# Layer 2: one block of W2 loaded as 96 rows in three padded groups and 32 rows apart

## The chip, the cores and the metric

The kernel runs on one core of a Trainium2 chip. The metric is device time in microseconds (us) of one execution. Runs of the kernel before: 1343.65, 1343.77 and 1344.35 us, median 1343.77 us.

## The reference

One token goes through two equal layers; each layer is attention over a cache of 8192 keys for 32 heads of 128, and then an MLP. All data is float32.

```
def _A_ref(x, k_cache, v_cache, wq, wo):
    q = (x @ wq).reshape(B, Sq, H, Dh).transpose(0, 2, 1, 3)      # H = 32, Dh = 128, D = 640
    scores = jnp.einsum("bhqd,bhkd->bhqk", q, k_cache) * (Dh ** -0.5)
    p = _softmax(scores, axis=-1)
    o = jnp.einsum("bhqk,bhkd->bhqd", p, v_cache)
    return o.transpose(0, 2, 1, 3).reshape(B, Sq, H * Dh) @ wo
def _B_ref(x, w1, w2):
    h = jnp.maximum(jnp.einsum("bsd,df->bsf", x, w1), 0)          # Dff = 1728
    return jnp.einsum("bsf,fd->bsd", h, w2)

x = x + _A_ref(_layernorm(x), A_k_cache, A_v_cache, A_wq, A_wo)
x = x + _B_ref(_layernorm(x), B_w1, B_w2)
x = x + _A_ref(_layernorm(x), A_k_cache, A_v_cache, A_wq, A_wo)
x = x + _B_ref(_layernorm(x), B_w1, B_w2)
```

## The kernel before

The caches do not fit in the on-chip memory, so nearly all of K and V is read from device memory twice, once per layer. The loads are issued from SP's queue, in an order written out by hand (UNITS, HEADS), into one large tile named ring. `pump` (from L179) issues the next load of K or V as soon as a place in the ring is free; `release` frees a place once TensorE has used it. The weights wq and wo come over ACT's queue.

The second weight matrix of the MLP, W2, is cut by rows into 14 blocks: blocks 0 to 12 are 128 rows by 640 columns (2560 bytes in each row), and block 13 (FB - 1) is packed into 128 rows by 320. `W2_LOADS` groups the blocks into transfers, one list for each layer. In the second layer (index 1 in the code) there are six: blocks 4, 5, 6; blocks 0 to 3; blocks 7, 8, 9; blocks 10, 11; block 12; block 13. `pump` issues them after the last piece of K and V, through `part_of_w2` (from L218), and they all go to SP's queue, so they are the last bytes that the kernel loads. Each has 128 rows.

A transfer waits before its issue for a semaphore named DMAHW0 to DMAHW7. There are eight, used in turn, so a transfer waits until the one that last used its semaphore has landed.

The end of the program is the MLP of the second layer (`mlp`). The hidden values are turned into columns (hT), and then `product(b)` multiplies the column of one block by this block of W2: four matmuls over 128x160 (L482) for blocks 0 to 12, four at L935 for block 13. The profile counts each such matmul as two instructions. The order is that of `W2_LOADS`: seven blocks (4, 5, 6, 0, 1, 2, 3), then some small matmuls for the layer norm (L961, L969, L391), then 7, 8, 9, then one matmul for the spread (L404), then 10, 11, 12, 13. One VectorE operation (L998) adds up, and SP stores the result (L1045).

Of the kernel before, what the change touches and what calls it, by code (L numbers as in the profile page):

```python
# [15 lines left out]
P = 128  # L16
D = 640
# [80 lines left out]
def wide(kind, piece):  # L98

    return 4 * piece[2] * (1 if kind == "k" else DH) // 8  # L100


def size(u):
    return sum(wide(kind, piece) for _, kind, piece in UNITS[u[0]][u[1]])
# [6 lines left out]
FB = 4 * F_TILES + F_REST  # L111
SLOTS = 7
W2_UNITS = SLOTS * D // 8
W2_LOADS = [
    [(0, 1, 2, 3), (4, 5, 6), (7,), (8, 9, FB - 1), (10,), (11,), (12,)],
    [(4, 5, 6), (0, 1, 2, 3), (7, 8, 9), (10, 11), (12,), (FB - 1,)],
]
W2_LAST = 2 * (F_ROWS[2] - P * F_TILES)
assert 2 * W2_LAST == P


def w2_width(blocks):
    return sum(D // 2 if b == FB - 1 else D for b in blocks)


@with_exitstack
def decode_kernel(ctx: ExitStack, tc: tile.TileContext, x, kv, wq, wo, wqo, w1, w2, out):
    nc = tc.nc
    consts = ctx.enter_context(tc.tile_pool(name="consts", bufs=1))
    wts = ctx.enter_context(tc.tile_pool(name="wts", bufs=1))  # L130
# [20 lines left out]
    dram_at, o = {}, 0  # L151
# [8 lines left out]
    def place(layer, u, n):  # L160


        step = 8 if u in KEPT else max(m for m in (8, 64, 256, 512) if n % m == 0)
        low, high = 0, FLAT if u[0] >= 28 else 3 * BIG
        if layer and (u[0] >= 28 or u[0] < HG):
            high = RING
        if n > FLAT // 3:
            step, high = BIG, 3 * BIG
        if layer == 0 and u in kept and (u in KEPT or u[0] == 30 and UNITS[30][u[1]][0][1] == "k"):
            low, high = (EDGE, RING) if u in KEPT else (FLAT, EDGE)  # L170
        at, best = low, None
        for a, m in sorted(live.values()) + [(high, 0)]:
            a = min(a, high)
            if a - at >= n and (best is None or a - at < best[1]):
                best = at, a - at
            at = max(at, -(-(a + m) // step) * step)
        return None if best is None else best[0]

    def pump():  # L179
        while todo:  # L180
            layer, u = todo[0]
            n = size(u)
            at = place(layer, u, n)
            if at is None:
                return
            todo.pop(0)
            o = dram_at[u]
            stays = PARK_ROW if (layer, u) == (1, PARKED) else 0
            nc.sync.dma_start(
                ring[:, 8 * at + stays : 8 * (at + n)],  # L190
                kv[o : o + 8 * P * n].rearrange("(p m) -> p m", p=P)[:, stays:],
            )
            if stays:
                for a, bank in parked:
                    nc.scalar.copy(ring[:, 8 * at + a : 8 * at + a + bank.shape[1]], bank)
            for t, (_, kind, piece) in enumerate(UNITS[u[0]][u[1]]):
                m = wide(kind, piece)
                live[layer, u, t] = at, m
                at_of[layer, u, t] = ring, 8 * at
                at += m  # L200
            if not todo or layer < todo[0][0]:
                assert all(a + m <= RING for a, m in live.values())
                live["w2"] = RING, W2_UNITS
                for part in W2_LOADS[layer][:2]:
                    part_of_w2(layer, part, by_parts[:, part[0] * D :])
                if layer == 0:
                    part_of_w2(0, W2_LOADS[0][2], wct.rearrange("p c d -> p (c d)"))
        rest = W2_LOADS[1][2:]
        if (1, rest[0][0]) not in w2_block:
            n = w2_width(sum(rest, ()))  # L210
            at = place(1, (0, None), n // 8)
            if at is not None:
                at *= 8
                for part in rest:
                    part_of_w2(1, part, ring[:, at:])
                    at += w2_width(part)

    def part_of_w2(L, blocks, where):  # L218
        loads = W2_LOADS[L]
        o = P * w2_width(sum(loads[: loads.index(blocks)], ()))  # L220
        n = w2_width(blocks)
        nc.sync.dma_start(where[:, :n], w2[L, o : o + P * n].rearrange("(p m) -> p m", p=P))
        at = 0
        for b in blocks:
            m = w2_width((b,))
            w2_block[L, b] = where[:, at : at + m]
            at += m
# [20 lines left out]
    def release(L, u, t):  # L248
        if (L or u not in kept) and at_of[key(L, u, t)][0] is ring:
            del live[key(L, u, t)]  # L250
            pump()
        if (L, u, t) in lent:
            lent.remove((L, u, t))
            if not lent:
                del live["w2"]
                pump()
# [35 lines left out]
    load_wq(0, nc.sync)  # L292
    nc.scalar.dma_start(xr, x)
    pump()
    load_wo(0, 0, nc.sync)

# [12 lines left out]
    blocks = ident.rearrange("p (g r) -> p g r", g=4)[:, :, :4]  # L309
# [574 lines left out]
    def mlp(L, o, last, xp, ph):  # L884
# [43 lines left out]
        def product(b):  # L928
# [4 lines left out]
            for g in range(4):  # L933
                rows = slice(W2_LAST * (g // 2), W2_LAST * (g // 2 + 1))
                nc.tensor.matmul(  # L935
                    po[32 * g : 32 * g + 32, :DR],
                    hT[rows, b : b + 1].to_broadcast([W2_LAST, 32]),
                    wt[rows, g % 2 * DR : (g % 2 + 1) * DR],
# [117 lines left out]
def _hidden_rows():  # L1056

    b = [[F_AT[g] + j * P + np.arange(P) for g in range(4)] for j in range(F_TILES)]
    rest = [F_AT[g] + np.arange(F_TILES * P, F_ROWS[g]) for g in range(4)]
    blocks = [x for row in b for x in row]  # L1060
    blocks.append(np.concatenate(rest[:2]))
    blocks.append(np.concatenate(rest[2:] + [-np.ones(P - len(rest[2]) - len(rest[3]), int)]))
    return blocks


def _laid_out(A_x, A_k_cache, A_v_cache, A_wq, A_wo, B_w1, B_w2):
    k = np.asarray(A_k_cache)[0].reshape(H, 4, 4, RUN, DH).transpose(0, 4, 1, 2, 3)
    v = np.asarray(A_v_cache)[0].reshape(H, 4, 4, NBL, 4, 32, DH).transpose(0, 1, 5, 3, 4, 2, 6)
    v = v.reshape(H, P, NBL, 4, 4, DH)
    kv = np.empty(H * P * SK * 2, k.dtype)  # L1070
    o = 0
    for u in ORDER:
        n = 8 * size(u)
        block = kv[o : o + P * n].reshape(P, n)
        o += P * n
        a = 0
        for h, kind, piece in UNITS[u[0]][u[1]]:
            if kind == "k":
                r, c, m = piece
                part = k[h, :, :, r, c : c + m]  # L1080
            else:
                b, r, m = piece
                part = v[h, :, b, :, r : r + m]
            part = part.reshape(P, -1)
            block[:, a : a + part.shape[1]] = part
            a += part.shape[1]
    w2 = np.zeros((P, FB, D), np.asarray(B_w2).dtype)
    for b, f in enumerate(_hidden_rows()):
        w2[f >= 0, b] = np.asarray(B_w2)[f[f >= 0]][:, _COLS]
    w2[W2_LAST:, -1, : D // 2] = w2[:W2_LAST, -1, D // 2 :]  # L1090
    wq = np.asarray(A_wq).reshape(NB, P, NG, HG * DH).transpose(2, 1, 0, 3).reshape(NG, P, HG * D)
    wo = np.asarray(A_wo)[:, _COLS].reshape(NG, HG, DH, D).transpose(0, 2, 1, 3)
    wqo = [
        [np.concatenate([wq[b], wo[a].reshape(P, HG * D)], 1) for a, b in zip(gs[1:-1], gs[2:])]
        for gs in GROUPS
    ]
    return {
        "x": np.repeat(np.asarray(A_x).reshape(D)[_COLS].reshape(4, DR), 32, axis=0),
        "kv": kv,
        "wq": wq.reshape(NG * P, HG * D),  # L1100
        "wo": wo,
        "wqo": np.array(wqo),
        "w1": np.asarray(B_w1).reshape(NB, P, DFF).transpose(1, 0, 2),
        "w2": np.array(
            [
                np.concatenate(
                    [
                        np.concatenate([w2[:, b, : w2_width((b,))] for b in part], 1).reshape(-1)
                        for part in loads
                    ]  # L1110
                )
                for loads in W2_LOADS
            ]
        ),
    }


# [22 lines left out]
```

## Time and profile before

| what | value |
|---|---|
| runs | 1343.65, 1343.77, 1344.35 us |
| span of the profiled execution, first to last instruction | 1340.6 us |
| median of the runs less this span | 3.2 us |
| bytes read from device memory | 570.83 MB, 426 GB/s over the span |
| TensorE busy, VectorE busy | 65%, 22% of the span |
| the chain that ended last, by engine | DMA 67%, PE 27%, DVE 4% |

For the profiled execution the page gives the span and no separate total, so the 3.2 us stand for what lies around the span. The DMA share in a stretch is the mean busy share of the core's 16 DMA engines: 0.50 means that eight engines' worth of work was done. In a list of DMA issues the last number is the time from the issue to the landing of the whole transfer.

### The profile page before, as it was taken

To read this page: it belongs to the slowest core of one execution; us is meant where nothing else is said; L and a number is where in the kernel's file an instruction comes from. 1 tells how busy PE (TensorE), PEld (TensorE's weight loads), DVE (VectorE), ACT (ScalarE), POOL (GpSimd) and SP (SyncE) were. 2 spreads that over 40 slices of the span, in tenths; PEclk is the share of its full clock that TensorE was granted. 3 is DMA by queue.
4 is the path that set the end of the run, shared out by engine and by line. 5 is a ranking of instruction groups with operands and counts; after the bars stand their busy time and mean duration, and the time that the engine had idled before them with its cause. 6 is when DMAs were issued, how large, how long until landed. Compare 5 with 4: busy or idle time off the path is not lost.

```text
span 1340.6 us, 13403 instructions
## 1 busy us (share of the span) xinstructions
PE 874.0 (65%) x5806; PEld 255.5 (19%) x5806; DVE 290.2 (22%) x956; ACT 62.6 (5%) x155; POOL 2.9 (0%) x10
## 2 busy tenths in 40 slices
PE   5463575767657656676688755657566666567687
PEld 2110121111111111112243211112111111111123
DVE  2120121211212112223123212221221212212222
ACT  0000000000000000000000000000000000000000
POOL 0000000000000000000000000000000000000000
PEclk8686787988777887788799977887778787888789
DMA  9999999999999999999999999999999999999998
GB/s 395 431 435 430 442 423 437 429 428 437 432 434 429 428 439 426 433 425 415 425 396 425 430 435 433 432 433 431 433 429 434 432 428 433 437 427 436 425 424 333
DMA packets 24546, 571.70 MB, mean 426 GB/s; under 512 B 2724, under 2 KB 2984, under 8 KB 6952
## 3 DMA queue, kind: packets, MB, share of 16 engines
q1 hardware_dynamic: 21464, 529.31, 92.1%
q10 hardware_dynamic: 3024, 41.53, 7.3%
q8 instruction: 46, 0.75, 0.2%
q14 instruction: 12, 0.10, 0.0%
HBM read 570.83 MB, written 0.00 MB: 426 GB/s over the span
## 4 chain that ended last, share of the span: by engine, by line
DMA 67%; PE 27%; DVE 4%; ACT 1%; issue 1%; SPq 0%; ACTq 0%; DVEq 0%
DMA ring<-in_kv 66%; PE ps L516 10%; PE outs L570 9%; PE side L672 1%; DMA ring<-in_w 1%; DVE p L591 1%; PE acc L621 1%; PE side L440 1%; ACT p L545 1%; DVE h_t L531 1%; PE small L536 1%; PE small L604 1%; PE side L454 1%; DVE p L552 0%; DVE h_t L537 0%
## 5 line engine op out<-in xcount | busy, mean ns | idle before, releaser
L516 PE MATMUL ps<-ring,spread_q 128*32 128x512 f32 (+3 forms) x2088 | 332.7, 727 | 149.2 <-DMA ring<-in_kv 148.6
L570 PE MATMUL outs<-ring,p 128*4 128x512 f32 (+3 forms) x2080 | 310.6, 732 | 164.1 <-DMA ring<-in_kv 95.7
L531 DVE TENSOR_REDUCE h_t<-ps 128x1 f32<-128x512 f32 x64 | 44.3, 691 | 365.4 <-PE ps L516 365.4
L570 PEld LDWEIGHTS outs<-ring,p 128*4 128x4 f32 x2080 | 50.6, 95 | 348.4 <-issue 233.8
L516 PEld LDWEIGHTS ps<-ring,spread_q 128*32 128x32 f32 x2088 | 63.9, 124 | 277.5 <-issue 188.8
L545 ACT ACTIVATE p<-ps,h_t 128x512 f32<-128x512 f32 x63 | 43.3, 687 | 1161.2 <-DVE h_t L537 1161.2
L552 DVE STREAM_TRANSPOSE p<-p 128x128 f32<-128x128 f32 x256 | 79.8, 312 | 63.9 <-ACT p L545 57.2
L587 DVE TENSOR_SCALAR p<-outs,ind 128x128 f32<-128x128 f32 x64 | 22.5, 351 | 317.2 <-PE outs L570 317.2
L604 PE MATMUL small<-ones,p 128*128 128x1 f32 (+1 forms) x128 | 25.3, 267 | 97.4 <-DVE p L591 97.4
L591 DVE SCALAR_TENSOR_TENSOR p<-outs,ind,p 128x128 f32<-128x128 f32 x188 | 66.0, 351 | 6.7
L536 PE MATMUL small<-ident,h_t 128*128 128x128 f32 x128 | 32.7, 339 | 40.1 <-DVE h_t L531 39.9
L604 PEld LDWEIGHTS small<-ones,p 128*128 128x128 f32 x128 | 19.9, 195 | 159.7 <-DVE p L591 158.9
L672 PE MATMUL side<-w_t,wct 128*128 128x448 f32 (+1 forms) x80 | 45.3, 651 | 0.0
L452 DVE TENSOR_SCALAR q_row<-side,ln_r 128x128 f32<-128x128 f32 x56 | 19.5, 349 | 106.0 <-PE ps L516 59.0
L440 PE MATMUL side<-both_t,ln_xc 128*32 128x512 f32 x140 | 37.3, 844 | 0.0
L536 PEld LDWEIGHTS small<-ident,h_t 128*128 128x128 f32 x128 | 20.0, 196 | 89.0 <-DVE h_t L531 85.5
L621 PE MATMUL acc<-both_t,o_cols 128*64 128x320 f32 x220 | 34.6, 458 | 0.0
L454 PEld LDWEIGHTS side<-sel,q_row 128*128 128x128 f32 x112 | 19.3, 216 | 56.3 <-DVE q_row L452 29.9
L537 DVE TENSOR_REDUCE h_t<-small 128x1 f32<-128x128 f32 x64 | 18.7, 292 | 35.4 <-PE small L536 35.4
L454 PE MATMUL side<-sel,q_row 128*128 128x1 f32 x112 | 24.1, 284 | 0.3 <-DVE q_row L452 0.2
L621 PEld LDWEIGHTS acc<-both_t,o_cols 128*64 128x64 f32 x220 | 15.5, 147 | 29.4 <-issue 17.7
L672 PEld LDWEIGHTS side<-w_t,wct 128*128 128x128 f32 x80 | 13.5, 211 | 32.4 <-issue 32.4
(148 smaller groups left out, 219.5 us busy)
## 6 DMA issues: line engine op xcount, KB each, us to landing
ring<-in_kv SPq DMA_DIRECT2D x50, 6144.0 KB, 35.0
ring<-in_kv SPq DMA_DIRECT2D x23, 4096.0 KB, 33.2
ring<-in_kv SPq DMA_DIRECT2D x29, 2048.0 KB, 27.7
both_t<-in_wqo ACTq DMA_DIRECT2D x12, 2560.0 KB, 24.7
ring<-in_kv SPq DMA_DIRECT2D x4, 5120.0 KB, 34.6
ring<-in_kv SPq DMA_DIRECT2D x9, 1024.0 KB, 23.9
w_t<-in_w ACTq DMA_DIRECT2D x1, 4320.0 KB
ring<-in_kv SPq DMA_DIRECT2D x5, 768.0 KB, 29.5
```

The source lines that it names most:

```text
L440: nc.tensor.matmul(pq[32 * strip : 32 * strip + 32], xc[:, c : c + 1].to_broadcast([P, 32]), wq_t[:, c], start=c < 4, stop=c in (1, 2, 3, ...
L454: nc.tensor.matmul(mine[:, :1], row, one_of_each, start=True, stop=True, skip_group_check=True)
L516: nc.tensor.matmul(hd.ps[32 * g : 32 * g + 32, c : c + n], spread_q[:, 3 - r : 35 - r], tile_of[:, at + g * n : at + (g + 1) * n], start=f ...
L531: nc.vector.tensor_reduce(hd.nm, hd.ps, AX.X, ALU.max, negate=True)
L536: nc.tensor.matmul(pt[:, :P], hd.nm.to_broadcast([P, P]), ident, start=True, stop=True)
L545: nc.scalar.activation(hd.p, hd.ps, AF.Exp, bias=hd.low, scale=scale, accum_out=hd.l)
L552: nc.vector.transpose(hd.all_p[:, b * P : (b + 1) * P], hd.p[:, b * P : (b + 1) * P])
L570: nc.tensor.matmul((hd.out if r0 < 2 else hd.out_2)[32 * g : 32 * g + 4, r0:r1].rearrange("p r d -> p (r d)"), hd.all_p[:, 32 * i : 32 * i ...
L591: nc.vector.scalar_tensor_tensor(oc, hd.out[:, r], ind[:, r : r + 1], oc, op0=ALU.mult, op1=ALU.add)
L604: nc.tensor.matmul(pt[:, :n], part, mask.to_broadcast([P, n]), start=i == 0, stop=i == len(parts) - 1,)
L621: nc.tensor.matmul(acc[64 * g : 64 * g + 64, : 2 * DR], col.to_broadcast([P, 64]), wt[:, 2 * DR * g : 2 * DR * (g + 1)], start=first, stop ...
L672: nc.tensor.matmul(pt[:, :n], wct[:, c], w1_t[:, c, f : f + n], start=(c == 0), stop=(c == NB - 1),)
```

## The change

The first transfer of layer 2's W2 (blocks 4, 5, 6) is cut into block 4 alone and blocks 5, 6. Block 4 is then loaded by two transfers. The first carries rows 0 to 95, from a new array w2_front of three lines; each line holds 32 rows and 64 padding values, so that the lines do not run into one another and the source has three as its outermost size. The second carries rows 96 to 127. Destination, values and the order of the products stay the same. `W2_FIRST` says how many transfers go to the fixed place: two in layer 1, three in layer 2.

```
 W2_LOADS = [
     [(0, 1, 2, 3), (4, 5, 6), (7,), (8, 9, FB - 1), (10,), (11,), (12,)],
-    [(4, 5, 6), (0, 1, 2, 3), (7, 8, 9), (10, 11), (12,), (FB - 1,)],
+    [(4,), (5, 6), (0, 1, 2, 3), (7, 8, 9), (10, 11), (12,), (FB - 1,)],
 ]
+W2_FIRST = [2, 3]
+FRONT = 3
+FRONT_ROWS = 32 * FRONT
+FRONT_GAP = 64
...
-                for part in W2_LOADS[layer][:2]:
+                for part in W2_LOADS[layer][: W2_FIRST[layer]]:
                     part_of_w2(layer, part, by_parts[:, part[0] * D :])
...
-        nc.sync.dma_start(where[:, :n], w2[L, o : o + P * n].rearrange("(p m) -> p m", p=P))
+        if L and blocks == loads[0]:
+            nc.sync.dma_start(
+                where[:FRONT_ROWS, :n],
+                w2_front[:, : 32 * n].rearrange("g (r m) -> g r m", m=n),
+            )
+            o += FRONT_ROWS * n
+            nc.sync.dma_start(
+                where[FRONT_ROWS:, :n],
+                w2[L, o : o + (P - FRONT_ROWS) * n].rearrange("(p m) -> p m", m=n),
+            )
+        else:
+            nc.sync.dma_start(where[:, :n], w2[L, o : o + P * n].rearrange("(p m) -> p m", p=P))
...
+    front = np.zeros((FRONT, 32 * D + FRONT_GAP), w2.dtype)
+    front[:, : 32 * D] = w2[:FRONT_ROWS, first].reshape(FRONT, 32 * D)
```

SP's queue at the end of the program, before: the last two pieces of V (1536 and 512 values in each row), the six transfers of W2 (in_w) and the store. The semaphore that each waits for stands in brackets.

```order
L189 DMA ring<-in_kv 128x1536 [waits DMAHW2_49,PE_49]
L189 DMA ring<-in_kv 128x512 [waits DMAHW3_49,PE_49]
L222 DMA ring<-in_w 128x1920 [waits DMAHW4_49]
L222 DMA ring<-in_w 128x2560 [waits DMAHW5_49]
L222 DMA ring<-in_w 128x1920 [waits DMAHW6_49,PE_49]
L222 DMA ring<-in_w 128x1280 [waits DMAHW7_49,PE_49]
L222 DMA ring<-in_w 128x640 [waits DMAHW0_49]
L222 DMA ring<-in_w 128x320 [waits DMAHW1_49]
```

The same place in the changed program, whose lines are numbered some 4 to 15 higher:

```order
L193 DMA ring<-in_kv 128x1536 [waits DMAHW2_49,PE_49]
L193 DMA ring<-in_kv 128x512 [waits DMAHW3_49,PE_49]
L227 DMA ring<-in_w_front 96x1x640 [waits DMAHW4_49]
L232 DMA ring<-in_w 32x640 [waits DMAHW5_49]
L237 DMA ring<-in_w 128x1280 [waits DMAHW6_49]
L237 DMA ring<-in_w 128x2560 [waits DMAHW7_49]
L237 DMA ring<-in_w 128x1920 [waits DMAHW0_49,PE_49]
L237 DMA ring<-in_w 128x1280 [waits DMAHW1_49,PE_49]
L237 DMA ring<-in_w 128x640 [waits DMAHW2_49]
L237 DMA ring<-in_w 128x320 [waits DMAHW3_49]
```

There are eight transfers of W2 where there were six. The last two now wait for the semaphores DMAHW2 and DMAHW3, which the last two pieces of V use, where they waited for DMAHW0 and DMAHW1.

TensorE in the MLP of layer 2, before: the seven early blocks and the three after them (side is the accumulator, hT the columns of hidden values).

```order
L482 MATMUL side<-ring,hT 32x160 [waits DMAHW4_49,DVE_49]
L482 MATMUL side<-ring,hT 32x160 x11
L482 MATMUL side<-ring,hT 32x160 [waits DMAHW5_49]
L482 MATMUL side<-ring,hT 32x160 x15
L961 MATMUL acc<-sel,by_act 64x1 [waits PE_49,Activation_49]
```

The same place in the changed program:

```order
L497 MATMUL side<-ring,hT 32x160 [waits DMAHW5_49,DMAHW4_49,DVE_49]
L497 MATMUL side<-ring,hT 32x160 x3
L497 MATMUL side<-ring,hT 32x160 [waits DMAHW6_49]
L497 MATMUL side<-ring,hT 32x160 x7
L497 MATMUL side<-ring,hT 32x160 [waits DMAHW7_49]
L497 MATMUL side<-ring,hT 32x160 x15
L976 MATMUL acc<-sel,by_act 64x1 [waits PE_49,Activation_49]
```

No matmul moves. The first product waits for two transfers in place of one, and the product of block 5 has a wait of its own.

## Rows read from the trace of the kernel before

**Rows 1.** The page: span, the queues of instruction and data packets, the chain's shares.

```profile
span 1340.6 us, 13403 instructions
...
q1 hardware_dynamic: 21464, 529.31, 92.1%
...
q8 instruction: 46, 0.75, 0.2%
...
DMA 67%; PE 27%; DVE 4%; ACT 1%; issue 1%; SPq 0%; ACTq 0%; DVEq 0%
```

**Rows 2.** The chain that ended last, from 1315 us: start, us, what.

```profile
1316.50 19.15 DMA ring<-in_w
...
1335.70 0.75 PE side L482 x16
...
1336.49 0.48 PE side L482 x8
1336.97 0.45 PE side L935 x8
...
1337.55 0.38 DVE xr L998
```

**Rows 3.** SP's issues in order of time: start, us, engine, line, what.

```profile
1296.94 0.33 SPq L189 DMA_DIRECT2D ring<-in_kv  x1
...
1301.78 0.33 SPq L222 DMA_DIRECT2D ring<-in_w  x1
...
1316.50 0.33 SPq L222 DMA_DIRECT2D ring<-in_w  x1
1321.43 0.33 SPq L222 DMA_DIRECT2D ring<-in_w  x1
1323.86 0.33 SPq L222 DMA_DIRECT2D ring<-in_w  x1
1337.96 0.65 SPq L1045 DMA_DIRECT2D out<-xr  x1
```

**Rows 4.** DMA issues in windows around five of these: KB, us to landing.

```profile
ring<-in_kv SPq DMA_DIRECT2D x1, 256.0 KB, 29.5
ring<-in_w SPq DMA_DIRECT2D x1, 960.0 KB, 27.0
ring<-in_w SPq DMA_DIRECT2D x1, 640.0 KB, 19.2
ring<-in_w SPq DMA_DIRECT2D x1, 320.0 KB, 15.0
ring<-in_w SPq DMA_DIRECT2D x1, 160.0 KB, 13.0
```

**Rows 5.** Windows at the end: the last three columns are clock, DMA share, GB/s.

```profile
1316.00:1326.00 10.00, 8.75 (x106) 3.35 (x106) 2.40 (x7) 0.78 (x2) 0.00 (x0) 1.00 1.00 411
...
1331.00:1331.50 0.50, 0.24 (x5) 0.15 (x9) 0.17 (x1) 0.00 (x0) 0.00 (x0) 1.00 0.93 379
1331.50:1332.75 1.25, 1.25 (x41) 1.19 (x40) 0.00 (x0) 0.00 (x0) 0.00 (x0) 1.00 0.66 268
1332.75:1335.50 2.75, 2.74 (x64) 2.01 (x52) 1.02 (x6) 0.00 (x0) 0.00 (x0) 1.00 0.53 212
1335.50:1336.00 0.50, 0.31 (x10) 0.29 (x13) 0.16 (x1) 0.00 (x0) 0.15 (x1) 1.00 0.22 79
1336.00:1336.50 0.50, 0.46 (x18) 0.14 (x6) 0.00 (x0) 0.00 (x0) 0.40 (x1) 1.00 0.04 15
```

**Rows 6.** TensorE's matmuls in order of time, in the last MLP.

```profile
1331.36 2.11 PE L482 MATMUL side<-ring,hT 128*32 128x160 f32 x56 [0.26 <-DVE hT L922]
...
1334.18 1.02 PE L482 MATMUL side<-ring,hT 128*32 128x160 f32 x24
1335.13 0.38 PE L404 MATMUL small<-ln_ss,sel 128*128 128x1 f32 x2
```

**Rows 7.** Instructions of line 482 from 1330 us: duration ns min/median/max.

```profile
L482 PEldq EVENT_SEMAPHORE  x1: 51/51/51, 1330.6 to 1330.6; - x1
```

More of the change, by code (lines that the diff above doesn't have):

```diff
@@ L126, in decode_kernel @@
 @with_exitstack
-def decode_kernel(ctx: ExitStack, tc: tile.TileContext, x, kv, wq, wo, wqo, w1, w2, out):
+def decode_kernel(ctx: ExitStack, tc: tile.TileContext, x, kv, wq, wo, wqo, w1, w2, w2_front, out):
     nc = tc.nc
@@ L207, in pump @@
                     part_of_w2(0, W2_LOADS[0][2], wct.rearrange("p c d -> p (c d)"))
-        rest = W2_LOADS[1][2:]
+        rest = W2_LOADS[1][W2_FIRST[1] :]
         if (1, rest[0][0]) not in w2_block:
@@ L1090, in _laid_out @@
     w2[W2_LAST:, -1, : D // 2] = w2[:W2_LAST, -1, D // 2 :]
+    first = W2_LOADS[1][0][0]
+    front = np.zeros((FRONT, 32 * D + FRONT_GAP), w2.dtype)
+    front[:, : 32 * D] = w2[:FRONT_ROWS, first].reshape(FRONT, 32 * D)
     wq = np.asarray(A_wq).reshape(NB, P, NG, HG * DH).transpose(2, 1, 0, 3).reshape(NG, P, HG * D)
@@ L1114, in _laid_out @@
         ),
+        "w2_front": front,
     }
```

## Prediction

> **What bounds the kernel now.** The page comes first: a span of 1340.6 us, and a chain of waits that is 67% DMA [rows 1]. The share of the data queue, 92.1% of all 16 engines' time, says why: the kernel is a stream of loads, and the work of TensorE and VectorE lies beside it. The change touches only the last transfers, so the rest is read from the end of the trace. The chain there has one long link, a transfer of W2, and behind it only short ones: 16 matmuls at 1335.70, 8 at 1336.49, 8 at 1336.97 and one VectorE operation at 1337.55 [rows 2]. The first three each begin when a transfer has landed. From issue and time to landing: blocks 10 and 11 at 1316.50 + 19.2 = 1335.7, block 12 at 1321.43 + 15.0 = 1336.4, block 13 at 1323.86 + 13.0 = 1336.9 [rows 3, 4]. So the landing of the last W2 bytes sets the end, and from there 1340.6 - 1336.9 = 3.7 us remain that the change does not touch.
>
> Why does the stream end at 1336.9? The windows show it. Until 1331.0 all engines are busy. Then the share falls to 0.93, 0.66 and, from 1332.75 to 1335.5, to 0.53, then 0.22 and 0.04 [rows 5]. Each engine has the same number of data bytes, for every load has 128 rows. Yet some 16 x (1 - 0.53) = 7.5 engines have nothing left by 1332.75, while 8 or 9 go on until 1335.5 to 1336.5. The reader is to see two groups, about 4 us apart. What is left after 1331.0 is 0.5 x 0.93 + 1.25 x 0.66 + 2.75 x 0.53 + 0.5 x 0.22 + 0.5 x 0.04 = 2.9 us of all 16 engines. Shared out evenly it would be over at 1333.9, 2.6 us earlier than 1336.5: no shift of bytes can give more than that here, 0.19% of the time.
>
> One thing that could set engines back is the traffic of instructions: 46 packets, 0.75 MB [rows 1], 16 KB each. That they fall on some engines only is a guess; the profile gives no engine numbers.
>
> **The change part by part.** *The bytes moved.* Block 4 is 128 rows of 2560 bytes. Spread over 16 engines that is 8 rows, 20,480 bytes, for each. Afterwards 96 rows lie in three groups, 32 rows (81,920 bytes) for each of three engines, and the other 32 rows give 2 rows (5,120 bytes) to all. Thirteen engines have 15,360 bytes less, three have 66,560 bytes more. An engine moves 411 / 16 = 25.7 GB/s where the share is 1.00 [rows 5]. So the thirteen finish 15,360 / 25.7e3 = 0.60 us earlier, and the three finish 66,560 / 25.7e3 = 2.59 us later. If the three belong to the early group, they end at some 1331.0 to 1332.75, plus 2.6, at the latest 1335.4; the late group ends at 1336.5 - 0.6 = 1335.9 and still sets the end. The gain is then 0.60 us.
>
> *What TensorE can take of it.* The transfers would land at 1335.1, 1335.8 and 1336.3. L404 starts at 1335.13 and takes 0.38 us [rows 6], and waits for no transfer, so blocks 10 and 11 can begin at 1335.5 rather than 1335.7. At the pace of the seven early blocks, 56 matmuls in 2.11 us, 0.038 us each [rows 6], the 24 matmuls of blocks 10 to 12 take 0.9 us, and block 13 begins at 1336.4; it began near 1336.9. That leaves 0.5 us of the 0.60. I take 0.5.
>
> *That three engines are used* is not shown by any row of before, where every load has 128 rows. I take it from the code: a source of three lines against a destination of 96 rows. [...] No run here shows it so far. The other end is that the 96 rows spread over all 16, and then nothing moves: 0 us.
>
> *Block 4's own landing.* Its product is the first. Layer 2's W2 starts behind the last piece of V, which lands at 1296.94 + 29.5 = 1326.4 [rows 3, 4]. On the latest engine 34 rows then take 87,040 / 25.7e3 = 3.4 us, to 1329.8. TensorE comes to it at 1331.36, held by VectorE's hT [rows 6]. So 1.5 us of cover hide it; before, it landed at 1301.78 + 27.0 = 1328.8 [rows 3, 4]. Without the cover it would cost at most the 1.0 us between the two.
>
> *Two more issues on SP.* An issue takes 0.33 us [rows 3], and SP has nothing else to do here. But the semaphores are used in turn, so each transfer from blocks 7 to 9 on is issued when a transfer two places later than before has landed. The last, block 13, now waits for the last piece of V and goes out at 1326.4, not at 1323.86. From an issue into an empty queue to the end of everything the store takes 1340.6 - 1337.96 = 2.6 us [rows 1, 3], so the descriptors are there by 1329.1 at the latest, and the first engine runs dry at 1331.0 less 0.6 = 1330.4. It costs nothing while this 1.3 us of cover stands, and even an early engine that starved has about 3 us to spare.
>
> *One more wait on TensorE.* The first product waits for two transfers; a semaphore instruction there took 51 ns [rows 7], and block 5 gets a wait too. Between 0 and 0.1 us, in a stretch before blocks 7 to 9 (1334.18), whose end TensorE does not set. Behind the waiting matmul stand all 56, and VectorE for the layer norm after them, but by 1331.36 blocks 4 to 6 have landed. I take 0.
>
> **Sum.** Nothing before 1326.4 changes. 1340.6 - 0.5 = 1340.1 us of span; with 3.2 us around the span (median 1343.77 less 1340.6) 1343.3 us.
>
> **The rivals.** *One of the three engines is late (slower).* The mechanism is the same, the place is the end of its data. Engines of the late group end between 1335.5 and 1336.5 [rows 5]; plus 2.59 this gives 1338.1 to 1339.1 against 1336.5, so 1.6 to 2.6 us later, 1345.4 to 1346.4 us, as a point 1345.9. It decides from the moment that one of the three is less than 2.6 us ahead of the last: an engine dry by 1335.9 - 2.6 = 1333.3 leaves the gain whole, one dry by 1333.9 costs nothing, a later one is a loss. For it: half the engines are late, and no row says which. Three drawn by lot from 16 would nearly always include a late one. Against it: the share falls by half within 1.75 us and then stays level, as for two blocks of eight, and if the blocks go by number, three neighbours lie in one of them. [...]
>
> *Nothing moves.* The 96 rows spread over 16 engines, or the last engine is held by something else, a late instruction packet: 1343.8 us. For it: no load on fewer engines is in the trace of before. Against it: the padding makes the source three lines.
>
> *The later issues starve the queue (slower).* If block 13 took its 13.0 us from 1326.4, it would land at 1339.4, 2.6 us later: 1346.4 us. Against it: these 13.0 us are queueing behind other loads, for 160 KB over 16 engines take 0.4 us.
>
> **How the numbers follow.** The forecast, early engines, 0.50 (1343.3; its own range 1342.7 to 1343.8). A late engine among the three 0.33 (1345.4 to 1346.4). Nothing moves 0.12 (1343.8). Starved 0.05 (1346.4). The runs of before lie 0.7 us apart, which is the slack that I give below. The range 1342.5 to 1346.1 leaves out the top third of the late case, most of the starved one and a little below: 0.11 + 0.04 + 0.02 = 0.17. About 0.2%, 2.7 us, is what a measurement of this kernel can tell from no change. Faster than 1341.1 is beyond the bound of 2.6 us: 0.03, for a different layout of data. Slower than 1346.5: the top of two cases and mishaps, 0.09. The rest, 0.88, is no difference, whichever way the three engines lie.
>
> **What the profile after would show.** Right: a shorter tail in the windows, with the share still near 1 to about 1330.5 and then *higher* than 0.53 for two or three us; the last W2 landing about 0.6 us nearer to the last piece of V's landing; L935 at about 1336.4. The transfer of 240 KB should take 3 us or more of an engine behind that piece. Wrong: a share that falls to 3/16 = 0.19 and stays there for 1 to 2 us at the very end, with L482 and L935 waiting for it, means that late engines carry the front; an unchanged tail means that it was spread; a hole in the share between 1326 and 1330 means starved queues. What makes me wrong altogether is which engines are late, and that the trace of before does not say.

## The result, and the profile after

The changed kernel takes 1345.55 us (median of 20 runs), the kernel before 1343.59 us (20 runs beside them): 1.96 us more by the medians, ratio 1.0024, 95% interval [1.0015, 1.0033]. The ratio, here and below, goes with the means (1347.12 and 1343.93 us), which lie 3.2 us apart. Of the 20 runs of the changed kernel 12 took 1344.5 to 1345.9 us and 8 took 1348.3 to 1351.5; what follows explains the 2 us of the medians, and what makes the 8 is open. The time lies in the range of the prediction (1342.5 to 1346.1), but on the other side of no change: slower, where 1343.3 was forecast.

One thing has to be known to read the profile after. Its execution took 1349.95 us, and by the end it runs about 6 us late: TensorE's granted clock was 0.50 between 700 and 712 us, where before had 1.00. In the 4 us ahead of that TensorE was busy 2.63 us, in before 3.58. This lies far ahead of the first changed instruction. So its end is compared with the end of before by distances, not by the clock on the wall. The page:

```profile
span 1348.2 us, 13405 instructions
...
q1 hardware_dynamic: 21611, 529.31, 91.9%
...
DMA 62%; PE 31%; DVE 4%; ACT 1%; issue 1%; SPq 0%; ACTq 0%; DVEq 0%
```

The bytes are the same as in [rows 1]; there are two instructions and 147 data packets more. The packets tell how many engines the front uses, which the prediction could not read. The counts fit one packet for each row of a transfer and one for each of its engines: of the kernels below, split_only has 144 more than before (128 rows, 16 engines) and front16 160 (128 rows, twice 16 engines). The 147 here are 128 rows, 16 engines for the 32 rows, and 3 for the front; the pages fit this, for 19 of the 147 are under 512 bytes (2743 such packets, 2724 before). The chain that ended last, from 1298 us (start, us, what), answers to [rows 2]:

```profile
1298.92 34.77 DMA ring<-in_kv
1333.69 0.14 issue
1333.83 0.62 PE outs L585 x8
...
1339.17 2.11 PE side L497 x56
...
1341.98 0.95 PE side L497 x24
...
1343.32 0.68 PE side L497 x16
...
1344.00 0.48 PE side L497 x8
1344.48 0.45 PE side L950 x8
```

The long link has changed. It was a transfer of W2, up to 1335.7; now it is a piece of K or V (in_kv), and from its landing on TensorE's chain runs with hardly a gap to the last block. TensorE no longer waits long for W2. It gets V late. W2 has not come early, either: the last transfer, block 13, lands at 1334.42 + 9.9 = 1344.3, just ahead of its product at 1344.48. SP's issues (start, us, engine, line, what), as [rows 3]:

```profile
1302.96 0.33 SPq L193 DMA_DIRECT2D ring<-in_kv  x1
...
1307.80 0.90 SPq L227 DMA_DIRECT2D ring<-in_w_front  x1
1312.69 0.35 SPq L232 DMA_DIRECT2D ring<-in_w  x1
1317.58 17.16 SPq L237 DMA_DIRECT2D ring<-in_w  x6
...
1334.42 0.33 SPq L237 DMA_DIRECT2D ring<-in_w  x1
```

The last of these lines is the last of the six, block 13.

And the DMA issues in windows around these (KB, us to landing), as [rows 4]:

```profile
ring<-in_kv SPq DMA_DIRECT2D x1, 256.0 KB, 31.4
...
ring<-in_w SPq DMA_DIRECT2D x1, 640.0 KB, 11.8
ring<-in_w SPq DMA_DIRECT2D x1, 320.0 KB, 10.2
ring<-in_w SPq DMA_DIRECT2D x1, 160.0 KB, 9.9
```

The last piece of V, 256 KB, issued ahead of everything that the diff touches, took 31.4 us to land where it took 29.5: **1.9 us later**. It is not chance of one execution: the same piece took 31.2 and 32.1 us in front16 and far_source, which have the same slow stretch, and 29.5 in front_last, whose slow stretch comes behind V. From that landing to the end of the span there are 1348.2 - 1302.96 - 31.4 = 13.8 us, against 1340.6 - 1296.94 - 29.5 = 14.2 before: **0.3 us shorter**. Together +1.6 us in this execution; +1.96 by the medians. The later issues did not hurt: block 13 landed 9.9 us after its issue, where it took 13.0.

Why V landed late is in the windows of one us (the last three columns are clock, DMA share, GB/s), as [rows 5]:

```profile
1326.00:1327.00 1.00, 0.61 (x8) 0.00 (x0) 0.10 (x2) 0.78 (x2) 0.00 (x0) 1.00 0.99 386
1327.00:1328.00 1.00, 0.43 (x9) 0.25 (x12) 0.90 (x3) 0.00 (x0) 0.00 (x0) 1.00 1.14 325
1328.00:1329.00 1.00, 1.00 (x18) 0.52 (x14) 0.34 (x2) 0.00 (x0) 0.00 (x0) 1.00 0.95 259
1329.00:1330.00 1.00, 1.00 (x20) 0.48 (x16) 0.13 (x1) 0.00 (x0) 0.00 (x0) 1.00 1.07 271
1330.00:1331.00 1.00, 0.64 (x8) 0.00 (x0) 0.00 (x0) 0.00 (x0) 0.00 (x0) 1.00 0.97 250
1331.00:1332.00 1.00, 0.57 (x12) 0.36 (x16) 0.00 (x0) 0.00 (x0) 0.00 (x0) 1.00 1.08 271
1332.00:1333.00 1.00, 1.00 (x20) 0.27 (x8) 0.00 (x0) 0.00 (x0) 0.00 (x0) 1.00 1.02 337
1333.00:1334.00 1.00, 0.39 (x8) 0.14 (x8) 0.00 (x0) 0.00 (x0) 0.00 (x0) 1.00 1.00 353
...
1339.00:1340.00 1.00, 0.82 (x24) 0.80 (x28) 0.12 (x1) 0.00 (x0) 0.00 (x0) 1.00 0.80 332
1340.00:1341.00 1.00, 1.00 (x40) 0.92 (x30) 0.00 (x0) 0.00 (x0) 0.00 (x0) 1.00 0.72 296
1341.00:1342.00 1.00, 1.00 (x28) 0.74 (x22) 0.22 (x2) 0.00 (x0) 0.00 (x0) 1.00 0.68 273
```

Two columns have to be read together here. The share stays near 1: all 16 engines count as busy, and nothing starves. But for four us (1328 to 1332) they move 250 to 271 GB/s, and for three more 325 to 353, where before moved 411 at the same share [rows 5]. Against 410 the seven us from 1327 to 1334 are short of 85 + 151 + 139 + 160 + 139 + 73 + 57 = 804 GB/s x us, or 0.80 MB, which is 2.0 us of the stream: the size of the loss. At the end the share is 0.80, 0.72 and 0.68 where it was 0.66 and 0.53: what the prediction named as the sign that it was right, and yet the kernel is slower.

### The profile page after: what moved, and what is told of

Its sections match the earlier page's. It is cut to its first block, busy times and chain, and to the rows that moved or that the text cites. A ratio compares the mean times of both kernels' runs of the same rounds, so it can differ in the third digit from the quotient of the medians.

```text
span 1348.2 us, 13405 instructions
## 1 busy us (share of the span) xinstructions
PE 899.4 (67%) x5806; PEld 260.6 (19%) x5806; DVE 290.1 (22%) x956; ACT 62.5 (5%) x155; POOL 2.9 (0%) x10
## 2 busy tenths in 40 slices
DMA packets 24693, 571.70 MB, mean 424 GB/s; under 512 B 2743, under 2 KB 3003, under 8 KB 7099
## 4 chain that ended last, share of the span: by engine, by line
DMA 62%; PE 31%; DVE 4%; ACT 1%; issue 1%; SPq 0%; ACTq 0%; DVEq 0%
DMA ring<-in_kv 61%; PE ps L531 12%; PE outs L585 10%; ACT p L560 1%; DVE h_t L546 1%; PE side L455 1%; PE side L687 1%; PE small L551 1%; DVE p L606 1%; PE acc L636 1%; PE side L469 1%; DVE p L567 1%; DVE h_t L552 1%; PE small L619 1%; PE outs L424 1%
## 5 line engine op out<-in xcount | busy, mean ns | idle before, releaser
L585 PE MATMUL outs<-ring,p 128*4 128x512 f32 (+3 forms) x2080 | 334.4, 783 | 176.5 <-DMA ring<-in_kv 103.5
L531 PE MATMUL ps<-ring,spread_q 128*32 128x512 f32 (+3 forms) x2088 | 329.3, 720 | 118.5 <-DMA ring<-in_kv 118.1
```

The costliest lines, as they stand in the source:

```text
L531: nc.tensor.matmul(hd.ps[32 * g : 32 * g + 32, c : c + n], spread_q[:, 3 - r : 35 - r], tile_of[:, at + g * n : at + (g + 1) * n], start=f ...
L585: nc.tensor.matmul((hd.out if r0 < 2 else hd.out_2)[32 * g : 32 * g + 4, r0:r1].rearrange("p r d -> p (r d)"), hd.all_p[:, 32 * i : 32 * i ...
```

## The experiments

The first theory, A, was that the loss comes of three engines with much to do; its rivals, that it comes of more transfers (B), of the layout of the source (D), or of the rows that are written (E, later made sharper as F). extra24, extra12, own8 and other8 are the kernel before with one transfer more, ahead of W2, into memory that nothing reads; the others are the changed kernel with an edit. In each, a drop of the bytes at a full share is called a dip. Windows are of one us, columns as above.

**split_only**: block 4 apart from 5 and 6, but loaded by one transfer of 128 rows.

```
-        if L and blocks == loads[0]:
+        if False:
```

> Block 4 is a transfer of its own, but of 128 rows on sixteen engines; the rest is as in the changed kernel. Theory A (the transfer on three engines slows every engine while it lasts): the windows before the last W2 transfers stay near 410 GB/s at a share of 1, and the time is that of the kernel before, 1343.6 us within 0.5 us. Rival B (the cost is the extra transfer, its later issue times and waits): about 1345.0 to 1345.5 us without the front.

1343.56 us (11 runs) against 1343.36; ratio 0.9999, interval [0.999, 1.0007]. No window from 1322 to 1331 is under 387 GB/s. The transfer more, the later issues and the wait more on TensorE cost nothing that can be measured; B falls.

**front16**: the same 96 rows, read from W2 without padding, by all 16 engines (6 rows each).

```
-                w2_front[:, : 32 * n].rearrange("g (r m) -> g r m", m=n),
+                w2[L, o : o + FRONT_ROWS * n].rearrange("(p m) -> p m", m=n),
```

> The two transfers of 96 and 32 rows stay, but the 96 rows come from W2 itself as 96 lines, so sixteen engines share them, 6 rows each. Theory A: no slow stretch, time as before, 1343.6 us within 0.5 us. Rival C (any transfer whose rows do not fall on the engines as in a transfer of 128 rows slows the stream): a dip in GB/s for some 1 us, and 0.3 to 1 us more than before. Rival B: 1345.0 us or more.

1345.91 us (11 runs), ratio 1.0027, interval [1.0016, 1.0038]: as slow as the change, with no engine loaded more than another, and slower than C had said (0.3 to 1 us). The windows show two dips:

```profile
1322.00:1323.00 1.00, 0.63 (x12) 0.33 (x16) 0.93 (x3) 0.00 (x0) 0.00 (x0) 1.00 1.02 286
1323.00:1324.00 1.00, 1.00 (x18) 0.52 (x14) 0.48 (x3) 0.00 (x0) 0.00 (x0) 1.00 1.03 294
...
1328.00:1329.00 1.00, 0.87 (x23) 0.35 (x22) 0.37 (x2) 0.00 (x0) 0.00 (x0) 1.00 0.96 256
```

They stand some five us apart, about as far as the early and the late engines, so each group seems to come to the transfer in its own time. A, as stated, falls: it is not that three engines carry the rows.

**far_source**: the three lines of the source 1 MB apart.

```
-FRONT_GAP = 64
+FRONT_GAP = 262144
```

> As the changed kernel, but the three lines of the new array lie 1 MB further apart in device memory (padding of 262144 values for 64). Rival D (the three lines lie so near one another that their reads collide in device memory): the stretch at 250 to 270 GB/s goes, and the time falls to some 1343 us. Theory A, or a collision on the side of the on-chip memory: the dip stays at 250 to 270 GB/s for some 5 us, and the time stays near 1345.5 us.

1345.5 us (12 runs), ratio 1.0019, interval [1.001, 1.0028]; the dip is there, 252 to 290 GB/s for five us (1324 to 1329). D falls.

**extra24**: before, with 24 rows of 10,240 bytes on three engines.

```
+                if layer:
+                    nc.sync.dma_start(
+                        both_t[:24, : 4 * D],
+                        w2_front[:, : 32 * D].rearrange("g (r m) -> g r m", m=4 * D),
+                    )
```

> The kernel before with one transfer more, ahead of W2 in SP's queue: 240 KB on three engines into memory that nothing reads any more, as 24 rows of 10240 bytes in place of 96 rows of 2560. Theory E (what collides is the destination: 32 rows for each engine walk over the rows of many other engines): with 8 rows for each engine, the share of a normal transfer, the dip in GB/s is gone or much weaker (above 350 GB/s at a share of 1). If three engines or the new array by themselves are the cause: the dip is there, near 260 GB/s for 4 to 5 us.

One run, 1349.65 us. The dip is deeper than in the change:

```profile
1325.00:1326.00 1.00, 1.00 (x22) 0.68 (x22) 0.00 (x0) 0.00 (x0) 0.00 (x0) 1.00 1.04 216
1326.00:1327.00 1.00, 0.95 (x12) 0.15 (x4) 0.00 (x0) 0.00 (x0) 0.00 (x0) 1.00 0.94 211
```

So E falls in the form that it had here, in which engine e owns rows 8e to 8e + 7. Theory F keeps the idea without that form: a transfer slows all engines while an engine writes rows that another engine writes in the transfers of 128 rows. Which engine writes which row is in no trace. The next two runs therefore test only whether the place of the rows matters.

**own8** and **other8**: the same 240 KB from eight padded lines, four rows of 7,680 bytes from each, in rows 0 to 31 or in rows 64 to 95. The two differ in one number (64 for 0 in other8). That the eight lines go to eight engines is carried over from the 147 packets, where three lines fit three engines. F, as it was put to the test, expected a dip in other8 alone.

```
+                    nc.sync.dma_start(
+                        both_t[0 : 0 + 32, : 3 * D],
+                        w2_front[:, : 12 * D].rearrange("g (r m) -> g r m", m=3 * D),
+                    )
```

> The kernel before with one transfer more ahead of W2: 240 KB that nothing reads, from eight padded lines, 4 rows of 7680 bytes to each of eight engines, into rows 0 to 31. [...] If engine e writes rows 8e to 8e+7, or if any transfer on fewer than sixteen engines is harmful, there is a dip to 210 to 290 GB/s for some 3 us.

> The same transfer in all but the place: rows 64 to 95. [...] If the number of engines, the padding, the extra transfer or its source were the cause: the same windows as with rows 0 to 31.

One run of each: own8 1344.05, other8 1347.02, before 1343.35 us. Two windows of own8:

```profile
1326.00:1327.00 1.00, 1.00 (x24) 0.58 (x17) 0.00 (x0) 0.00 (x0) 0.00 (x0) 1.00 1.09 446
...
1328.00:1329.00 1.00, 0.56 (x20) 0.27 (x10) 0.70 (x2) 0.36 (x1) 0.00 (x0) 1.00 0.97 404
```

And of other8:

```profile
1323.00:1324.00 1.00, 1.00 (x18) 0.52 (x14) 0.34 (x2) 0.00 (x0) 0.00 (x0) 1.00 0.95 209
1324.00:1325.00 1.00, 1.00 (x20) 0.47 (x16) 0.14 (x1) 0.00 (x0) 0.00 (x0) 1.00 0.94 225
...
1329.00:1330.00 1.00, 0.61 (x20) 0.21 (x16) 0.55 (x2) 0.00 (x0) 0.00 (x0) 1.00 1.04 238
```

Bytes, source and issue (0.85 us) are the same; only the rows that are written differ. In the one case the stream is untouched, in the other it loses up to half of its rate, twice (209 and 238 GB/s, against 410). The two dips lie some five us apart, so the eight engines do not seem to be one group: some are early and some late. Both were timed again with more runs.

**own8_timed** and **other8_timed**: the same two kernels.

> [...] 240 KB more take 0.6 us of a full stream, and 30,720 bytes 1.2 us of each of the eight engines. Theory F: no dip, +0.6 to +1.2 us, 1344.0 to 1344.7. Rival (it was chance that one run showed no dip): +2 us or more, as other8.

> [...] Theory F: the stream falls to 210 to 300 GB/s for some 5 us in all, +3 to +4 us, 1346.3 to 1347.5. Rival: the same as own8_timed within 0.5 us.

own8_timed 1344.35 us (10 runs), ratio 1.0004, interval [0.9995, 1.0013]; other8_timed 1346.99 us (9 runs), ratio 1.0023, interval [1.0014, 1.0033]; before 1343.58 us (26 runs). The intervals do not touch, and the dips are where they were (202 and 261 GB/s in 1328 to 1330 for other8_timed, nothing under 384 in own8_timed before 1332). So the place of the rows matters, by 2.6 us, and both times are as F forecast.

**extra12**: as extra24, with 12 rows, four from each of the three lines, all within the rows 0 to 31 of own8.

```
+                        both_t[:12, : 4 * D],
+                        w2_front[:, : 16 * D].rearrange("g (r m) -> g r m", m=4 * D),
```

> The kernel before with one transfer more ahead of W2, that nothing reads: three padded lines, on three engines as in the changed kernel, but only rows 0 to 11, 4 rows of 10240 bytes (40 KB, 1.6 us) to each engine. Theory F (the harm is rows that another engine writes in a transfer of 128 rows): these are each engine's own rows, so no dip in GB/s, and since the three engines are among the early ones the tail does not move: last W2 landing some 10.4 us after the last piece of V, as before. If three engines or three lines are harmful as such: a dip to 210 to 290 GB/s for 1.5 us or more.

One run, 1343.58 us against 1343.56, and no dip (434 GB/s in 1325 to 1326, where extra24 had 216). So a transfer from three padded lines is not harmful as such. It has half the bytes of extra24; but own8, with all of extra24's bytes into rows 0 to 31, has no dip either. extra12 gives each of the three 40,960 bytes more, 1.6 us at 25.7 GB/s, and the end did not move in this run: the three seem to be early engines, as the prediction had assumed.

**rows32**: the changed kernel without the transfer of the 96 rows, which leaves them unloaded; the 32 rows on all 16 engines stay.

```
-            nc.sync.dma_start(
-                where[:FRONT_ROWS, :n],
-                w2_front[:, : 32 * n].rearrange("g (r m) -> g r m", m=n),
-            )
```

> The changed kernel with the three-engine transfer left out, so that rows 0 to 95 of block 4 are not loaded; only the 32 rows go, 2 rows to each of sixteen engines. [...] If only the three-engine transfer collides: no dip.

One run, 1343.49 us against 1343.56, with two small dips (376 to 379, and this one):

```profile
1326.00:1327.00 1.00, 1.00 (x18) 0.53 (x14) 0.00 (x0) 0.00 (x0) 0.00 (x0) 1.00 1.14 363
1327.00:1328.00 1.00, 1.00 (x28) 0.66 (x20) 0.30 (x1) 0.00 (x0) 0.00 (x0) 1.00 0.88 312
```

The 80 KB cost 31 + 33 + 34 + 32 + 47 + 98 = 275 GB/s x us against 410, some 0.7 us, and the 96 rows that are not loaded save 0.6 us: nothing is left of either. One run can't show 0.1 us; that the two cancel is an estimate from these windows.

**quarter4**: block 4 apart, 128 rows, of which only the first 160 columns are loaded, so that each engine has 15,360 bytes less (shared evenly over 16), and the rows are shared out as in the transfers of before.

```
-                where[:FRONT_ROWS, :n],
...
+                where[:, :DR], w2[L, o : o + P * n].rearrange("(p m) -> p m", p=P)[:, :DR]
```

> Block 4 apart, in 128 rows on sixteen engines, but only its first 160 of 640 columns, the other columns are not loaded: every engine has 15,360 bytes less, as the thirteen engines of the changed kernel, and no row changes hands. If the size of the gain in the prediction was right (0.60 us less on the last engines, 0.5 us of it left by TensorE): no dip, last W2 landing some 0.6 us nearer to the last piece of V, and 1343.0 us, which is at the limit of what the rounds can tell from 1343.5. If TensorE or something else sets the tail: the landing comes nearer, the time does not.

1343.0 us (11 runs) against 1343.56 (14 runs): -0.56 us by the medians, ratio 0.9994, interval [0.9985, 1.0004]. That is the size of the gain term, and the interval has 1 in it, so it can't be told from no change.

**front_last**: the change with block 4 issued behind all other W2 and multiplied last, when K and V have landed.

```
-                for part in W2_LOADS[layer][: W2_FIRST[layer]]:
+                for part in W2_LOADS[layer][layer : W2_FIRST[layer]]:
...
+                part_of_w2(1, W2_LOADS[1][0], by_parts[:, W2_LOADS[1][0][0] * D :])
...
+        if L:
+            early, late = early[1:], late + early[:1]
```

> The change, with block 4 (its 96 rows on three engines, and its 32 rows on all) issued behind all other transfers of W2 and multiplied last; nothing is left out. Theory F (a transfer slows the stream while it writes rows that other engines write) in its strict form, at any load: K and V keep 410 GB/s up to the end of their stream, but the three engines take 3.2 us (81,920 bytes at 25.7 GB/s) to 5 us (at the pace measured in the changed kernel) from about 1330.5, end at 1333.7 to 1335.5, and the late engines beside them are slowed to 0.6 for that time, 1 to 2 us: 1344.0 to 1345.5 us in all. If the slowing needs a full stream (the late engines alone fill half of it): the gain forecast at first, 0.5 us, now comes: 1342.8 to 1343.3 us. If one of the three is a late engine (the rival of the prediction): 1345.4 to 1346.4, with a share of 0.19 at the very end. In all cases no dip below 350 GB/s ahead of the last landing of K and V.

1344.89 us (11 runs) against 1343.58, ratio 1.001, interval [1.0002, 1.0019]. K and V are untouched (406 to 437 GB/s from 1326 to 1331). The dip has moved to the end, where only some of the engines still work:

```profile
1334.00:1335.00 1.00, 0.74 (x16) 0.64 (x19) 0.24 (x2) 0.00 (x0) 0.00 (x0) 1.00 0.74 237
1335.00:1336.00 1.00, 1.00 (x39) 0.95 (x34) 0.00 (x0) 0.00 (x0) 0.00 (x0) 1.00 0.76 200
1336.00:1337.00 1.00, 1.00 (x30) 0.72 (x18) 0.11 (x2) 0.00 (x0) 0.00 (x0) 1.00 0.81 225
1337.00:1338.00 1.00, 0.56 (x14) 0.46 (x17) 0.87 (x6) 0.00 (x0) 0.00 (x0) 1.00 0.72 173
```

The same place in before, in windows of one us:

```profile
1332.00:1333.00 1.00, 1.00 (x36) 0.96 (x32) 0.00 (x0) 0.00 (x0) 0.00 (x0) 1.00 0.58 242
1333.00:1334.00 1.00, 1.00 (x30) 0.71 (x20) 0.08 (x2) 0.00 (x0) 0.00 (x0) 1.00 0.59 242
```

The share is higher, because the early engines now have work; the bytes are fewer. At a share of 0.76 to 0.81 the engines move 200 to 225 GB/s, where before moved 242 at 0.58. So the slowing does not need a full stream, and at the end of the tail the move is not free either.

## Why the prediction was wrong

**The bound and the two groups: right.** The tail of before is as it was read, and in extra12 the three engines behave as members of the early group. The rival "one of the three is late", with a chance of 0.33, does not hold: its mark, a share of 0.19 at the very end, is absent, although its time, 1345.4 to 1346.4, was met. The range reaches up to 1346.1 for this rival's sake, so that it holds the measured time is luck. That the three are early was partly luck too: the argument for it was two blocks of eight by number, and the two dips of other8 speak against such blocks. It also took the three engines for neighbours, which no run shows. Sharing the 96 rows over all 16 engines would not have helped: front16 does so and is as slow (1345.91 us). "Nothing moves" falls with the higher share at the end, and "the later issues starve the queue" with the 9.9 us of block 13.

**That three engines are used: right,** by the 147 packets.

**The gain of 0.60 us, of which 0.5 is left: right in size, as far as can be told.** In the change the last W2 lands 1344.32 - 1334.36 = 9.96 us after the last piece of V, and in before 1336.86 - 1326.44 = 10.42 us: 0.5 us nearer, where the prediction had named some 0.6 as a sign. The end of the span, counted from the same landing, is 0.3 us shorter. quarter4 takes the same bytes off every engine and is 0.56 us faster by the medians, which is not clear of no change.

**Two issues more, one wait more, later issues: right, 0.** split_only has all of them and measures a ratio of 0.9999. One detail was missed: the issue of the three lines holds SP for 0.90 us, not 0.33. Nothing waits for it.

**Block 4's own landing: still hidden, but its cover moved.** No row shows the landing of the front. TensorE came to the product at 1339.17 without a long wait for it.

**The offset was mis-told, and did no harm.** The prediction put 3.2 us around the span; the profiled executions of the other kernels have 1.7 to 1.9 (split_only 1344.14 us for a span of 1342.4). The rest seems to be that the profiled execution of before was a quick one. Both numbers were used together, so the forecast of 1343.3 does not change.

**The step that failed: "Nothing before 1326.4 changes".** With it goes the assumption that the rates of [rows 5] stay, 25.7 GB/s in each engine, whoever writes which row. Early engines seem to have come to the front while the late ones were still at K and V (the prediction's own two groups, 4 us apart, said as much, and the slow stretch begins seven us ahead of V's landing), so that the two ran side by side; all engines together fell to 250 to 271 GB/s. The last piece of V landed 1.9 us later than in before, and the whole tail with it. The sum should have been -0.5 (with 0.3 seen in the trace after) and +2.0, not -0.5 alone.

**The cause**, as far as it is shown: it is the rows. own8 and other8 differ in the destination alone, by 64 rows, and by 2.6 us. With extra12 against extra24, and front16 against split_only, which differ in more than the rows, three pairs fit one reading, F: a transfer is harmless while each engine writes rows that it writes in the transfers of 128 rows too, and slows everything that runs beside it when it does not. In the change, by this reading, rows 0 to 31, 32 to 63 and 64 to 95 go to one engine each. No trace names the engine that writes a row: this part is the author's estimate, from the order of the source's lines and the 3 of the 147 packets.

What happens at those rows is not shown. What the runs show is how the twelve kernels divide. Without a dip are before, split_only and quarter4 (transfers of 128 rows alone), own8 (rows 0 to 31, four from each line) and extra12 (rows 0 to 11, four from each line). With one are the change, far_source and front_last (96 rows from three lines), front16 (96 rows, six to an engine), rows32 (rows 96 to 127, two to an engine), extra24 (rows 0 to 23, eight from each line) and other8 (rows 64 to 95, four from each line). Why all 16 engines slow down together, in the change to 250 of 411 GB/s (61%) at a share of 0.97, is open: no run tells one cause from another.

A version that beats both kernels was not found. Each of the four that load all of block 4 as 96 rows and 32 (the change, front16, far_source, front_last) lost 1.3 us or more by the medians, against 0.5 us that there is to gain.

## What to carry to other kernels

Before bytes are moved from one DMA engine to another, ask which rows they go to, and try the place by itself: 240 KB more in rows 0 to 31 cost 0.8 us by the medians (own8_timed), which is not clear of no change, and the same 240 KB in rows 64 to 95 cost 3.4 us (other8_timed). A transfer that the change "does not touch" can be touched all the same: the last piece of V, issued ahead of every changed instruction, landed 1.9 us later. So in a stream-bound kernel price the stream, not the transfer. And read the DMA share together with GB/s: here shares of 0.95 to 1.08 went with 250 to 271 GB/s, a slowed stream, and the share alone would have shown nothing.

## What the runs showed of the hardware

- The transfers with a dip took the rate of all engines from about 410 to 202 to 300 GB/s at a share near 1 (the change, front16, far_source, extra24, other8 and other8_timed), and in a tail of half load from 242 GB/s at 0.58 to 200 to 225 at 0.76 to 0.81 (before and front_last). Even 80 KB spread evenly over 16 engines (rows32) did it in its one run, down to 312.
- SP's issue of a transfer from three or eight padded lines took 0.85 to 0.91 us, of the other loads of V and W2 0.31 to 0.40.
- Where a dip makes TensorE wait, there can be a second price. In extra24 TensorE stood idle for one us (1327 to 1328), and in 1330 to 1331 its granted clock fell from 1.00 to 0.50, until the last matmuls. The window of the idle stretch, and one of those at the lower clock:

```profile
1327.00:1328.00 1.00, 0.00 (x0) 0.01 (x1) 0.00 (x0) 0.00 (x0) 0.00 (x0) 1.00 0.96 384
...
1340.00:1341.00 1.00, 1.00 (x17) 0.77 (x20) 0.80 (x4) 0.00 (x0) 0.00 (x0) 0.50 0.00 0
```

  The profiled execution of far_source has the same between 1333 and 1339, behind a stretch in which TensorE was busy 0.41 of a us. In these two the span ended 8.9 and 6.6 us after the last W2 had landed, where it was 3.7 us in before. A gap does not always bring it: in split_only TensorE was busy 0.19 of the us from 1322 to 1323, and the clock stayed at 1.00.
